# Second layer's vector work kept in two lists and split into halves; raw weight loads issued first in each slot

## Chip, cores and metric

One core of one Trainium2 chip runs the whole kernel. The metric is device time in microseconds, the median of several executions; lower is better. Engines are named as the profile names them: PE (TensorE matmuls) and PEld (its weight loads), DVE (VectorE), ACT (ScalarE), POOL (GpSimd), and SPq, the queue on SyncE that issues the transfers.

## What is computed

```python
# q, k, v: (4, 8, 576, 64); w_in (512, 2048), w_out (2048, 512)
# moe2: w_gate, w_val (512, 1536), w_out (1536, 512); all float32
ret = (scale * q @ k.T) * Dmat          # Dmat[i, j] = gamma_h ** (i - j) for i >= j, else 0
x = merge_heads(ret @ v)                # (2304, 512)
h = x @ moe_w_in
g = h * tanh(log1p(exp(min(h, 20))))    # for h > 20: h * tanh(h)
x = g @ moe_w_out                       # first layer
g, val = x @ w_gate, x @ w_val
out = (g * sigmoid(g) * val) @ w_out    # second layer
```

## The kernel before

The program has three parts. **Retention** runs over 20 steps of up to 128 positions and prepares the first weights beside it. **The first layer** runs over 96 slots (`slot`, line 570): six blocks of 384 tokens by 16 slices of the hidden width; block b and place i in it make slot s = 16 b + i. **The second layer** (lines 601 to 790) works on three data sets of 768 tokens, and on each in six units u, one for each pair of 128-wide slices of its hidden width.

Every float32 product is made of three matmuls on a high half (a rounded copy that ACT casts) and a low half (the rest, a subtract on DVE). This is why each operand costs a cast and a subtract.

A slot gives PE 12 matmuls of `g1` (bank `h`) and 12 of `g2`, the latter for the slot LAG = 4 earlier (they add up in four banks `acc`). ACT then makes Mish (`mish`) and the high half, DVE the low half (`halves`). In a block's places 12, 13 and 15, `split_hi` and `split_lo` make the parts `xs` of the next block's input. In place 3 of the next block `g2_out` copies the four `acc` banks out to `y`, two on ACT and two on DVE. Whatever follows in the slot comes last: `second(s)` (line 228).

`second` prepares the second layer's weights beside the first layer, in five-slot steps, one for each of 12 groups (gate or value of one pair), from slot PREP = 20 on. Stage 0 of `group` issues two raw loads (`rawg` or `rawv`), stage 1 rebiases, stage 2 joins words, stage 3 makes four combinations and stores three operands through tiles `c` (four buffers) to DRAM (`comb`), stage 4 stores the other four. `last` does the same for a row of the output weights (`rawf`): its load is issued in the group's stage-4 slot, behind the four stores, and its rebias (line 103, ACT and DVE) stands in the slot after that. All these transfers are issued by SP in program order; a store there waits for the subtract that fills its tile, and what stands behind it waits too.

The second layer multiplies with Strassen's scheme: seven products `t` (six matmuls each) for gate (z = 0) and seven for value (z = 1) make one unit of 14 steps. Two of the three banks `t` of a pass take more than one product, so a bank must be emptied on DVE or ACT (line 719, 758) before the next but one step writes it; there are only two buffers in `pha`:

```python
                p = t[tn]
                n = z * NG + c
...
                fins(FINS[c])
                if nexty and n >= 6:
                    next(nexty[0], None)
```

In the value pass, steps 2, 4, 5 and 6 each finish one quarter: DVE multiplies it into the gate (`sg`, line 734), ACT casts the high half, DVE subtracts the low half (`finish`, `halves`). The output matmuls `fa` (line 689, nine for each quarter) go into `ready`, which is handed to `finq` when the next unit begins; `fins` takes 3, 2, 3, 2, 3, 2, 3 of them after the seven steps of a pass, so 36 in a unit. A data set's seven operands `y` (Strassen's combinations of the first layer's output, split into high and low) are made by `ysteps`: for the first set in the first layer's last four slots, two steps a slot, and for the next ones in the last unit of the set before, one step after each product from n = 6 on. Each such step is one or two DVE instructions of 768 elements a partition and a cast of 768. Where y, `second` and the rest meet on an engine, the order of the program decides: engines work in order.

## Time and profile before

| | us |
|---|---|
| time, median of 3 runs (lowest, highest) | 959.03 (956.24, 960.19) |
| the profiled execution | 957.2 |
| its span | 955.4 |
| PE busy | 918.8 (96%) |
| DVE busy | 518.9 (54%) |
| ACT busy | 360.8 (38%) |
| POOL busy | 109.3 (11%) |

PE is the busiest engine, and the chain that ended last runs on it for 72% of the span. Busy shares are averages over the three parts; what PE waits for, and where, is in the rows below. [...]

### The profile page before, as it was taken

What the parts mean: (1) busy time and instruction counts of PE and PEld (TensorE: products, weight loads), DVE (VectorE), ACT (ScalarE), POOL (GpSimd) and SP (SyncE); (2) the same over time, 40 slices, a digit from 0 to 9 for tenths busy, and PEclk for the clock granted to TensorE, in tenths of its full rate; (3) what the DMA queues carried; (4) which work ended last, traced back from release to release, by engine and by line L of the source; (5) the groups of instructions that cost most, each with busy time, mean ns of one, the idle gap of its engine ahead of it and who ended that gap; (6) DMA issues with size and microseconds to landing.
All of it is one profiled execution on the core that took longest, in us unless ns stands there. A gap on an engine that the chain in (4) does not pass through costs nothing.

```text
span 955.4 us, 14669 instructions
## 1 busy us (share of the span) xinstructions
PE 918.8 (96%) x5684; PEld 869.6 (91%) x5684; DVE 518.9 (54%) x896; ACT 360.8 (38%) x731; POOL 109.3 (11%) x90
## 2 busy tenths in 40 slices
PE   8898999999999999998999999998999997999998
PEld 7777899999999899998999899987999995999997
DVE  3997796255666656556234444455544456544444
ACT  4776564344554444445334222223222223222221
POOL 3765443000100000000000000000000000000000
PEclk9999999999999999999999999999999999999999
DMA  9999453045555555564116755543645443644411
GB/s 230 257 254 235 133 161 98 1 143 166 182 172 190 181 194 179 174 191 149 45 67 246 242 206 210 198 154 110 220 156 159 167 159 98 220 167 154 157 64 67
DMA packets 115349, 156.57 MB, mean 164 GB/s; under 512 B 45392, under 2 KB 80976, under 8 KB 115280
## 3 DMA queue, kind: packets, MB, share of 16 engines
q1 hardware_dynamic: 114176, 155.21, 51.8%
q8 instruction: 45, 0.74, 0.3%
q10 hardware_dynamic: 1104, 0.42, 0.2%
q14 instruction: 24, 0.20, 0.1%
HBM read 122.58 MB, written 33.03 MB: 163 GB/s over the span
## 4 chain that ended last, share of the span: by engine, by line
PE 72%; DMA 9%; DVE 9%; ACT 4%; SPq 2%; issue 2%; POOL 1%; DVEq 0%; ACTq 0%
PE t L749 26%; PE h L510 15%; PE fa L689 15%; PE acc L544 15%; DMA k<-in_k_dram 3%; DMA rawf<-in_moe_w_out_dram 2%; DMA comb<-c 2%; DMA rawv<-in_moe_w_val_dram 1%; DVE y L619 1%; SPq L300 1%; DVE g L567 1%; ACT y L618 1%; DMA rawg<-in_moe_w_gate_dram 1%; DVE c L177 1%; DVE rawv L108 1%
## 5 line engine op out<-in xcount | busy, mean ns | idle before, releaser
L749 PE MATMUL t<-y,su 128*128 128x384 f32 x1512 | 308.5, 340 | 13.4 <-DVE v L719 4.7
L749 PEld LDWEIGHTS t<-y,su 128*128 128x128 f32 x1512 | 271.7, 188 | 40.1 <-DVE cv L719 7.1
L510 PE MATMUL h<-xs,u 128*128 128x384 f32 x1152 | 216.7, 337 | 3.8 <-DVE xs L250 3.2
L544 PE MATMUL acc<-g,u 128*128 128x384 f32 x1152 | 215.2, 336 | 2.4 <-ACT y L554 2.4
L510 PEld LDWEIGHTS h<-xs,u 128*128 128x128 f32 x1152 | 202.0, 189 | 5.3 <-DVE xs L250 4.2
L544 PEld LDWEIGHTS acc<-g,u 128*128 128x128 f32 x1152 | 201.6, 188 | 3.2 <-ACT y L554 2.7
L567 DVE TENSOR_TENSOR g<-m,g 128x384 fp32r<-128x384 f32 x96 | 53.7, 559 | 100.1 <-ACT g L566 98.6
L561 ACT ACTIVATE m<-h 128x384 f32<-128x384 f32 x96 | 46.7, 487 | 93.7 <-PE h L510 93.6
L726 ACT ACTIVATE sg<-sg 128x384 f32<-128x384 f32 x54 | 28.4, 525 | 98.8 <-DVE sg L719 98.8
L123 POOL TENSOR_TENSOR u<-raw,u 128x512 fp32r<-128x512 f32 x32 | 47.1, 1473 | 62.1 <-ACT u L122 60.3
L177 POOL TENSOR_TENSOR f<-rawf,f 128x256 fp32r<-128x256 f32 x24 | 23.0, 979 | 262.5 <-ACT f L176 262.5
L566 ACT CAST g<-m 128x384 fp32r<-128x384 f32 x96 | 49.4, 514 | 2.8 <-PE acc L544 0.2
L719 DVE TENSOR_TENSOR v<-t,p 128x384 f32<-128x384 f32 x36 | 20.0, 557 | 45.5 <-PE t L749 44.6
L719 DVE TENSOR_TENSOR u<-t,p 128x384 f32<-128x384 f32 x36 | 20.0, 557 | 44.7 <-PE t L749 43.2
L104 DVE TENSOR_SCALAR raw<-raw 128x512 uint32<-128x512 uint32 x32 | 37.7, 1178 | 0.0
L104 DVE TENSOR_SCALAR rawf<-rawf 128x512 uint32<-128x512 uint32 x12 | 5.2, 430 | 48.3 <-DMA rawf<-in_moe_w_out_dram 48.3
L734 DVE TENSOR_TENSOR sg<-sg,cv 128x384 f32<-128x384 f32 x54 | 30.2, 558 | 1.9
L122 ACT CAST u<-raw 128x512 fp32r<-128x512 f32 x32 | 21.2, 662 | 22.3 <-DVE raw L112 22.2
L103 ACT ACTIVATE rawf<-rawf 128x512 f32<-128x512 f32 x12 | 8.3, 689 | 56.5 <-DMA rawf<-in_moe_w_out_dram 56.5
L357 POOL TENSOR_TENSOR vs<-v,gv 128x512 f32<-128x512 f32 (+1 forms) x20 | 27.0, 1348 | 20.6 <-DMA v<-in_v_dram 16.2
L108 DVE SCALAR_TENSOR_TENSOR raw<-raw 128x512 uint32<-128x512 uint32 x32 | 26.2, 818 | 0.0
L112 DVE SCALAR_TENSOR_TENSOR raw<-raw 128x512 uint32<-128x512 uint32 x32 | 26.1, 816 | 0.0
(363 smaller groups left out, 1064.6 us busy)
## 6 DMA issues: line engine op xcount, KB each, us to landing
su<-comb SPq DMA_DIRECT2D x126, 512.0 KB, 3.3
comb<-c SPq DMA_DIRECT2D x84, 256.0 KB, 2.4
raw<-in_moe_w_in_dram SPq DMA_DIRECT2D x16, 512.0 KB, 4.8
raw<-in_moe_w_out_dram SPq DMA_DIRECT2D x16, 512.0 KB, 3.6
rawg<-in_moe_w_gate_dram SPq DMA_DIRECT2D x12, 512.0 KB, 6.7
rawf<-in_moe_w_out_dram SPq DMA_DIRECT2D x12, 512.0 KB, 4.8
rawv<-in_moe_w_val_dram SPq DMA_DIRECT2D x12, 512.0 KB, 6.2
find<-f SPq DMA_DIRECT2D x24, 256.0 KB, 2.4
```

The source lines that it names most:

```text
L104: nc.vector.tensor_scalar(lo, lo, 29, None, op0=ALU.logical_shift_right)
L108: nc.vector.scalar_tensor_tensor(lo, hi, 0x80000000, lo, op0=ALU.bitwise_and, op1=ALU.bitwise_or)
L123: nc.gpsimd.tensor_tensor(out=u[:, 1, :], in0=w, in1=u[:, 0, :].bitcast(F32), op=ALU.subtract)
L177: eng.tensor_tensor(out=c[:, 1, :], in0=x, in1=c[:, 0, :].bitcast(F32), op=ALU.subtract)
L510: nc.tensor.matmul(ps, lhsT=u[:, a, kk * 128:(kk + 1) * 128], rhs=s[:, e, :], start=(c == 0), stop=(c == n - 1),)
L544: nc.tensor.matmul(accs[b][d][:, :T], lhsT=u[:, a, d * 128:(d + 1) * 128], rhs=g[:, e, :], start=(i == 0 and c == 0), stop=(i == F1 - 1 an ...
L561: nc.scalar.activation(w, hs.pop(s), AF.Mish)
L566: nc.scalar.copy(out=g[:, 0, :], in_=x)
L567: nc.vector.tensor_tensor(out=g[:, 1, :], in0=x, in1=g[:, 0, :].bitcast(F32), op=ALU.subtract)
L689: nc.tensor.matmul(accs["f", b][m], lhsT=gs[u, e, h][:, x, m * 128:(m + 1) * 128], rhs=fu[2 * (u % PAIRS) + e][:, a, :], start=first, stop ...
L719: nc.vector.tensor_tensor(out=out_, in0=a, in1=b_, op=ALU.add)
L749: nc.tensor.matmul(p, lhsT=w[:, n % 2, a, kk * 128:(kk + 1) * 128], rhs=y[:, x, kk, :], start=begin and kk == 0 and (a, x) == (0, 0), stop ...
```

## The change

1. `second` skips places 3 and 14 of every block (list `free`): its steps move to later slots, and the last one goes from slot 82 to slot 90. In a slot, the stages run in the order of their number, so that a raw load comes ahead of stores, and a group's stages 1 and 2 come ahead of `last`'s stages 2 and 3.
2. In the second layer the multiply of steps 4 to 6, the cast and the low-half subtract go to a list `later`, and the next data set's y to a list `ahead`. After a step's bank is emptied and its `fa` matmuls are issued, up to two entries of `later` and one of `ahead` are issued; casts to a high half do not count.
3. y is made in halves of 384 elements a partition: 22 DVE instructions in place of 11. The first part (12 of them) stands in the unit before the last, the rest in the last unit's value pass and in the first four steps of the next unit. The temporary gets a tile of its own (`t2`) instead of one of the five `g`. For the first data set eight entries are issued in a slot.
4. A quarter's `fa` matmuls enter `finq` when its low half is issued, not when the next unit begins.

```diff
@@ -225,13 +225,20 @@
             for h in range(DM // KH):
                 put(x[:, h * KH:(h + 1) * KH], find[i][:, :, h * KH:(h + 1) * KH], f"f{i}_{h}", nc.gpsimd)
 
+    free = [s for s in range(PREP, NB * F1) if s % F1 not in (3, F1 - 2)]
+
     def second(s):
+        if s not in free:
+            return
+        now = []
         for n in range(2 * PAIRS):
-            t = s - PREP - 5 * n
+            t = free.index(s) - 5 * n
             if 0 <= t < 5:
-                group(n // 2, n % 2, t)
+                now.append((t, group, (n // 2, n % 2, t)))
             if 4 <= t < 8:
-                last(n, t - 4)
+                now.append((t - 4, last, (n, t - 4)))
+        for _, f, a in sorted(now, key=lambda x: x[0]):
+            f(*a)
 
     xt = {}
     x2t = {}
@@ -613,52 +620,58 @@
             nc.sync.dma_start(out=fu[i].bitcast(F32), in_=find[i])
 
 
-        def ysplit(n, c, x):
-            y = pools["y"].tile([128, 2, KT // 2, T], F32R, tag="y", name=f"y{n}_{c}")
-            nc.scalar.copy(out=y[:, 0], in_=x)
-            nc.vector.tensor_tensor(out=y[:, 1], in0=x, in1=y[:, 0].bitcast(F32), op=ALU.subtract)
-            ys[n, c] = y
 
         def ysteps(n):
             b = {(k + 1, e + 1): x2t[2 * n + e][:, 2 * k:2 * k + 2, :] for k in range(2) for e in range(2)}
+            tmp = pools["t2"].tile([128, 2, T], F32, tag="t2", name=f"t2_{n}")
 
             def minus(out_, a, b_):
-                nc.vector.tensor_tensor(out=out_, in0=a, in1=b_, op=ALU.subtract)
-
-            ysplit(n, 0, b[1, 1])
-            minus(b[1, 1], b[1, 2], b[1, 1])
-            yield
-            t2 = gp.tile([128, 2, T], F32R, tag="g", name=f"t2_{n}", bufs=LAG + 1).bitcast(F32)
-            minus(t2, b[2, 2], b[1, 1])
-            ysplit(n, 1, t2)
-            yield
-            ysplit(n, 2, b[2, 1])
-            minus(b[2, 1], b[2, 1], t2)
-            yield
-            minus(b[1, 2], b[2, 2], b[1, 2])
-            ysplit(n, 3, b[1, 2])
-            yield
-            ysplit(n, 4, b[1, 1])
-            yield
-            ysplit(n, 5, b[2, 1])
-            yield
-            ysplit(n, 6, b[2, 2])
-            yield
-
-        y0 = None
+                def half(k):
+                    nc.vector.tensor_tensor(out=out_[:, k], in0=a[:, k], in1=b_[:, k], op=ALU.subtract)
+                return [lambda k=k: half(k) for k in range(KT // 2)]
+
+            def split(c, x):
+                def high():
+                    y = pools["y"].tile([128, 2, KT // 2, T], F32R, tag="y", name=f"y{n}_{c}")
+                    nc.scalar.copy(out=y[:, 0], in_=x)
+                    ys[n, c] = y
+
+                def rest(k):
+                    y = ys[n, c]
+                    nc.vector.tensor_tensor(out=y[:, 1, k], in0=x[:, k], in1=y[:, 0, k].bitcast(F32), op=ALU.subtract)
+
+                return high, [lambda k=k: rest(k) for k in range(KT // 2)]
+
+            h0, r0 = split(0, b[1, 1])
+            h1, r1 = split(1, tmp)
+            h2, r2 = split(2, b[2, 1])
+            h3, r3 = split(3, b[1, 2])
+            h4, r4 = split(4, b[1, 1])
+            h5, r5 = split(5, tmp)
+            h6, r6 = split(6, b[2, 2])
+            t1 = minus(b[1, 1], b[1, 2], b[1, 1])
+            t2 = minus(tmp, b[2, 2], b[1, 1])
+            t3 = minus(b[1, 2], b[2, 2], b[1, 2])
+            t4 = minus(tmp, b[2, 1], tmp)
+            return [h0] + r0 + t1 + t2 + [h1] + t3 + r1 + t4, [[h2] + r2, [h3] + r3, [h4] + r4, [h5] + r5, [h6] + r6]
+
+        y0 = []
         for s in range(2, NS):
             slot(s)
             if s == NS - 5:
                 cr.close()
                 pools["y"] = ctx.enter_context(tc.tile_pool(name="yp", bufs=9, side="right", reuse_waits="tile"))
                 pools["sg"] = ctx.enter_context(tc.tile_pool(name="sg", bufs=5, side="right", reuse_waits="tile"))
+                pools["t2"] = ctx.enter_context(tc.tile_pool(name="t2", bufs=1, side="right", reuse_waits="tile"))
                 pools["sa"] = ctx.enter_context(tc.tile_pool(name="sa", bufs=SA, side="right", reuse_waits="tile"))
                 for n in range(SA):
                     stream(n)
-                y0 = ysteps(0)
+                ya, yb = ysteps(0)
+                y0 = ya + [f for fs in yb for f in fs]
             elif y0:
-                next(y0, None)
-                next(y0, None)
+                for f in y0[:8]:
+                    f()
+                y0 = y0[8:]
         for s in range(NS - LAG, NS):
             g2(s)
             g2_out(s)
@@ -673,8 +686,9 @@
 
 
         sg = {}
-        ready = []
         finq = []
+        later = []
+        ahead = []
 
         def fins(count):
             while count and finq:
@@ -702,12 +716,23 @@
         def finish(u, e, h):
             i = u % PAIRS
             k = (e, h)
-            halves(sg.pop((u, e, h)), (u, e, h))
             start = i == 0 and k in ((0, 0), (1, 1))
             stop = i == PAIRS - 1 and k in ((1, 0), (0, 1))
-            lst = order(TT, stop)
-            for n, (m, a, x, c) in enumerate(lst):
-                ready.append((u, e, h, m, a, x, start and c == 0, stop and c == 2))
+
+            def high():
+                x = sg[u, e, h]
+                gs[u, e, h] = gp.tile([128, 2, T], F32R, tag="g", name=f"g{u}_{e}{h}", bufs=LAG + 1)
+                nc.scalar.copy(out=gs[u, e, h][:, 0, :], in_=x)
+
+            def rest():
+                x = sg.pop((u, e, h))
+                g = gs[u, e, h]
+                nc.vector.tensor_tensor(out=g[:, 1, :], in0=x, in1=g[:, 0, :].bitcast(F32), op=ALU.subtract)
+                for m, a, d, c in order(TT, stop):
+                    finq.append((u, e, h, m, a, d, start and c == 0, stop and c == 2))
+
+            later.append(high)
+            later.append(rest)
 
 
         def strassen(u, z):
@@ -731,7 +756,10 @@
                         x = pools["sg"].tile([128, T], F32, tag="cv", name=f"cv{u}_{e}{h}", bufs=2)
                         add(x, bank_, part_)
                     y = sg[u, e, h]
-                    nc.vector.tensor_tensor(out=y, in0=y, in1=x, op=ALU.mult)
+                    if part_ is None:
+                        nc.vector.tensor_tensor(out=y, in0=y, in1=x, op=ALU.mult)
+                    else:
+                        later.append(lambda: nc.vector.tensor_tensor(out=y, in0=y, in1=x, op=ALU.mult))
                     finish(u, e, h)
 
             for c, (nm, tn, begin, end) in enumerate((
@@ -771,22 +799,29 @@
                 else:
                     result(0, 1, p, r["u"])
                 fins(FINS[c])
-                if nexty and n >= 6:
-                    next(nexty[0], None)
+                k = u % PAIRS * 2 * NG + n - (PAIRS - 1) * 2 * NG - 8
+                if 0 <= k < 5 and u + 1 < NS2:
+                    ahead.extend(yb[k])
+
+                for todo_, m in ((later, 2), (ahead, 1)):
+                    while todo_ and m:
+                        f = todo_.pop(0)
+                        f()
+                        m -= f.__name__ != "high"
 
         FINS = (3, 2, 3, 2, 3, 2, 3)
         for u in range(NS2):
-            finq += ready
-            ready.clear()
-            nexty = []
-            if u % PAIRS == PAIRS - 1 and u + 1 < NS2:
-                nexty.append(ysteps(u // PAIRS + 1))
+            i = u % PAIRS
+            if i == PAIRS - 2 and u + 2 < NS2:
+                ya, yb = ysteps(u // PAIRS + 1)
+                ahead += ya
             if u + 1 < PAIRS:
                 fin_load(2 * u + 2)
                 fin_load(2 * u + 3)
             for z in range(2):
                 strassen(u, z)
-        finq += ready
+        while later:
+            later.pop(0)()
         fins(len(finq))
```

In the stage-4 slot of the group whose output row is `rawf5`, SP's queue had these rows (`c2_8` to `c2_13` are the four tiles of stage 4, `c2_7` to `c2_12` ahead of them the three of stage 3):

```order
L178 DMA comb2_3_89<-c2_7_3430 128x512
L178 DMA comb2_4_90<-c2_9_3434 128x512
L178 DMA comb2_6_92<-c2_12_3438 128x512
L178 DMA comb2_4_90<-c2_8_3472 128x512
L178 DMA comb2_5_91<-c2_10_3476 128x512
L178 DMA comb2_5_91<-c2_11_3480 128x512
L178 DMA comb2_6_92<-c2_13_3484 128x512
L171 DMA rawf5_3488<-in_moe2_w_out_dram 128x1024
L171 DMA rawg3_0_3522<-in_moe2_w_gate_dram 128x4x256
```

and has now:

```order
L178 DMA comb2_3_89<-c2_7_3559 128x512
L178 DMA comb2_4_90<-c2_9_3563 128x512
L178 DMA comb2_6_92<-c2_12_3567 128x512
L171 DMA rawf5_3601<-in_moe2_w_out_dram 128x1024
L178 DMA comb2_4_90<-c2_8_3603 128x512
L178 DMA comb2_5_91<-c2_10_3607 128x512
L178 DMA comb2_5_91<-c2_11_3611 128x512
L178 DMA comb2_6_92<-c2_13_3615 128x512
L171 DMA rawg3_0_3649<-in_moe2_w_gate_dram 128x4x256
```

The load of `rawf5` has moved ahead of four stores; the loads of the next group stay behind them.

On DVE, the value pass of unit 5 (the last of the first data set), from the emptying `u5_1` of step 1 to the emptying `cv5_01` of step 6; `y` on the left of an arrow is an operand or a combination of the next data set. Before:

```order
L719 TENSOR_TENSOR u5_1_6433<-t5_1_2_6426,p15_1_6416 128x384
L619 TENSOR_TENSOR y1_2_6437<-y2_3556,y1_2_6437 128x768
L626 TENSOR_TENSOR y2_3556<-y2_3556,t2_1_6421 128x768
L734 TENSOR_TENSOR sg5_00_6348<-sg5_00_6348,t5_1_1_6407 128x384
L567 TENSOR_TENSOR g(5, 0, 0)_6450<-sg5_00_6348,g(5, 0, 0)_6450 128x384
L626 TENSOR_TENSOR y3_4237<-y3_4237 128x768
L619 TENSOR_TENSOR y1_3_6457<-y3_4237,y1_3_6457 128x768
L719 TENSOR_TENSOR v5_1_6466<-t5_1_2_6426,p15_1_6416 128x384
L619 TENSOR_TENSOR y1_4_6470<-y2_3556,y1_4_6470 128x768
L719 TENSOR_TENSOR cv5_11_6482<-t5_1_3_6473,v5_1_6466 128x384
L734 TENSOR_TENSOR sg5_11_6372<-sg5_11_6372,cv5_11_6482 128x384
L567 TENSOR_TENSOR g(5, 1, 1)_6485<-sg5_11_6372,g(5, 1, 1)_6485 128x384
```

and now:

```order
L744 TENSOR_TENSOR u5_1_6465<-t5_1_2_6458,p15_1_6453 128x384
L641 TENSOR_TENSOR y1_2_6469<-y2_3516,y1_2_6469 128x384
L760 TENSOR_TENSOR sg5_00_6389<-sg5_00_6389,t5_1_1_6444 128x384
L730 TENSOR_TENSOR g5_00_6484<-sg5_00_6389,g5_00_6484 128x384
L641 TENSOR_TENSOR y1_2_6469<-y2_3516,y1_2_6469 128x384
L744 TENSOR_TENSOR v5_1_6494<-t5_1_2_6458,p15_1_6453 128x384
L641 TENSOR_TENSOR y1_3_6498<-y3_4179,y1_3_6498 128x384
L744 TENSOR_TENSOR cv5_11_6510<-t5_1_3_6501,v5_1_6494 128x384
L762 TENSOR_TENSOR sg5_11_6413<-sg5_11_6413,cv5_11_6510 128x384
L730 TENSOR_TENSOR g5_11_6516<-sg5_11_6413,g5_11_6516 128x384
L641 TENSOR_TENSOR y1_3_6498<-y3_4179,y1_3_6498 128x384
L744 TENSOR_TENSOR cv5_10_6526<-t5_1_2_6458,p15_1_6453 128x384
```

Between two emptyings there is now one instruction of 384 for the next set where there were one or two of 768, and the rest of these instructions has moved to the units on either side.

On PE, the value pass of unit 0, its steps 2 to 5 (`t0_1_*` are the products, `g(0, 0, 0)` or `g0_00` is the quarter that step 2 finishes). Before:

```order
L749 MATMUL t0_1_1_5474<-y0_2_5249,su4_5387 128x384 x6
L749 MATMUL t0_1_2_5485<-y0_3_5254,su5_5389 128x384 x6
L749 MATMUL t0_1_3_5514<-y0_4_5287,su5_5389 128x384 x6
L749 MATMUL t0_1_2_5485<-y0_5_5290,su6_5391 128x384 x6
L749 MATMUL t0_1_3_5514<-y0_6_5323,su6_5391 128x384 x6
L749 MATMUL t1_0_1_5559<-y0_0_5210,su7_5393 128x384 x6
```

and now:

```order
L777 MATMUL t0_1_1_5488<-y0_2_5260,su4_5401 128x384 x6
L777 MATMUL t0_1_2_5499<-y0_3_5294,su5_5403 128x384 x6
L703 MATMUL fa0_0_5528<-fu0_5411,g0_00_5517 128x512 x2
L777 MATMUL t0_1_3_5533<-y0_4_5298,su5_5403 128x384 x6
L703 MATMUL fa0_1_5529<-fu0_5411,g0_00_5517 128x512 x2
L703 MATMUL fa0_2_5530<-fu0_5411,g0_00_5517 128x512
L777 MATMUL t0_1_2_5499<-y0_5_5302,su6_5405 128x384 x6
L703 MATMUL fa0_2_5530<-fu0_5411,g0_00_5517 128x512
```

The `fa` matmuls of a quarter stand one product behind it, where they had stood behind the whole unit.

## Rows read from the trace of the kernel before

**Rows 1.** The page's busy time, share of the span and count for each engine.

```profile
PE 918.8 (96%) x5684; PEld 869.6 (91%) x5684; DVE 518.9 (54%) x896; ACT 360.8 (38%) x731; POOL 109.3 (11%) x90
```

**Rows 2.** The page's groups, PE: busy, mean ns | idle before, what ended it.

```profile
L749 PE MATMUL t<-y,su 128*128 128x384 f32 x1512 | 308.5, 340 | 13.4 <-DVE v L719 4.7
...
L510 PE MATMUL h<-xs,u 128*128 128x384 f32 x1152 | 216.7, 337 | 3.8 <-DVE xs L250 3.2
L544 PE MATMUL acc<-g,u 128*128 128x384 f32 x1152 | 215.2, 336 | 2.4 <-ACT y L554 2.4
```

**Rows 3.** Windows of 25 us: busy by engine, then clock, DMA share, GB/s.

```profile
300.00:325.00 25.00, 22.57 (x121) 21.72 (x120) 15.70 (x31) 11.85 (x28) 2.93 (x4) 0.95 0.48 158
325.00:350.00 25.00, 25.00 (x144) 25.00 (x143) 16.89 (x33) 12.10 (x27) 3.02 (x3) 0.98 0.53 179
...
650.00:675.00 25.00, 23.78 (x115) 21.74 (x115) 13.21 (x23) 6.93 (x13) 0.00 (x0) 0.93 0.41 137
```

**Rows 4.** Timeline of PE where data sets change: start, us, instruction [idle before <-releaser].

```profile
649.72 1.99 PE L749 MATMUL t<-y,su 128*128 128x384 f32 x6 [2.37 <-DVE v L719]
```

**Rows 5.** The same timeline at the second change of data sets.

```profile
797.41 1.31 PE L749 MATMUL t<-y,su 128*128 128x384 f32 x6 [2.36 <-DVE v L719]
```

**Rows 6.** Timeline of PE in the first layer, where a block's banks are emptied.

```profile
320.81 3.07 PE L544 MATMUL acc<-g,u 128*128 128x384 f32 x12 [2.37 <-ACT y L554]
```

**Rows 7.** Timeline of SPq, DVE, PE and ACT just ahead of that.

```profile
307.62 1.09 DVE L177 TENSOR_TENSOR c<-rawv,c 128x256 fp32r<-128x256 f32 x3
...
312.00 2.25 PE L510 MATMUL h<-xs,u 128*128 128x384 f32 x12
...
312.92 0.44 SPq L171 DMA_DIRECT2D rawf<-in_moe_w_out_dram  x1
...
318.76 0.69 ACT L103 ACTIVATE rawf<-rawf 128x512 f32<-128x512 f32 x1 [5.84 <-DMA rawf<-in_moe_w_out_dram]
```

**Rows 8.** The tile rawf: flight of its 12 loads, from issue to landing.

```profile
DMA to landing us min/median/max: 3.7/4.8/6.0
```

**Rows 9.** ACT's waits from 150 to 526 us: total, times, longest.

```profile
ACT rawf L103 <- DMA rawf<-in_moe_w_out_dram: 56.5, 12, 6.0
ACT c L176 <- DMA comb<-c: 24.5, 28, 5.0
```

**Rows 10.** Groups by shape on DVE: y's low half (768), the quarters' low half (384).

```profile
L567 DVE TENSOR_TENSOR g<-m,g 128x384 fp32r<-128x384 f32 x96 | 53.7, 559 | 100.1 <-ACT g L566 98.6 <-PE h L510 1.5
...
L619 DVE TENSOR_TENSOR y<-y,y 128x768 fp32r<-128x768 f32 x18 | 17.1, 956 | 6.9 <-ACT y L618 6.8
```

**Rows 11.** Timeline of an undisturbed unit's value pass, steps 2 and 3.

```profile
593.13 1.22 PE L749 MATMUL t<-y,su 128*128 128x384 f32 x6
...
594.98 0.51 ACT L566 CAST g(3, 0, 0)_6063<-sg 128x384 fp32r<-128x384 f32 x1 [3.39 <-DVE sg L734]
595.52 0.56 DVE L567 TENSOR_TENSOR g(3, 0, 0)_6063<-sg,g(3, 0, 0)_6063 128x384 fp32r<-128x384 f32 x1 [0.58 <-ACT g(3, 0, 0)_6063 L566]
595.77 0.19 PEld L689 LDWEIGHTS fa<-fu,g(2, 1, 0)_5917 128*128 128x128 f32 x1
```

**Rows 12.** The same unit, steps 4 to 6 and the next unit's step 1.

```profile
597.66 0.56 DVE L719 TENSOR_TENSOR cv<-t,v 128x384 f32<-128x384 f32 x1 [0.96 <-PE t L749]
...
599.39 0.56 DVE L567 TENSOR_TENSOR g(3, 1, 1)_6091<-sg,g(3, 1, 1)_6091 128x384 fp32r<-128x384 f32 x1 [0.58 <-ACT g(3, 1, 1)_6091 L566]
...
599.87 0.55 DVE L719 TENSOR_TENSOR cv<-t,p 128x384 f32<-128x384 f32 x1
...
602.07 0.55 DVE L719 TENSOR_TENSOR cv<-t,u 128x384 f32<-128x384 f32 x1
...
603.20 1.04 PE L749 MATMUL t<-y,su 128*128 128x384 f32 x5
```

**Rows 13.** Timeline of SPq: loads of the output weights; below it their flight.

```profile
515.71 1.75 SPq L613 DMA_DIRECT2D fu<-find  x4
```

**Rows 14.** The tile fu: flight of its 12 loads.

```profile
DMA to landing us min/median/max: 3.6/5.2/7.1
```

## Prediction

> **What bounds the kernel now.** I read the busy shares first: PE works for 918.8 of 955.4 us [rows 1], so what can be won is PE's idle time and its slow stretches, and the next view is what PE waited for. In the page's groups the second layer's products `t` wait 13.4 us in all, for DVE; the first layer's `h` waits 3.8 us, mostly for `xs`, and its `acc` 2.4 us for a copy by ACT [rows 2]. The rest of PE's idle time lies in the retention part, which the change does not touch. The windows of 25 us then tell what the clock lost: 0.95 and 0.98 behind the wait for `acc`, 0.93 at the first change of data sets [rows 3], so 25 x 0.07 = 1.75 us at each of the two places. The clock had fallen behind a wait of 2.37 us, where six matmuls then took 1.99 us [rows 4]; behind one of 2.36 us at the second change they took 1.31 [rows 5], so such a wait brings the fall only at times. An undisturbed unit shows DVE ending a chain in time, and no wait on PE [rows 11, 12]. So the waits sit in two places: where the next data set's y is made inside a value pass, and where the first layer's blocks change.
>
> **Second layer: waits that go.** The waits of `t` lie at the two changes of data sets [rows 4, 5] and, a small part, in unit 0's value pass, whose steps carry no `fa` matmuls before and now carry some. At the changes the cause is the same each time: an emptying of a bank stands on DVE behind a low half of 768 elements, itself behind a cast. The change leaves one half of 384 between two emptyings at most, and puts 12 of a set's 22 halves into a unit that had no such work. I take away 13.4 us. Six matmuls behind a wait take 1.31 to 1.33 us and 1.22 otherwise [rows 5, 11]; eleven waits make 11 x 0.1 = 1.1 us. With the waits goes what the clock lost behind them, 1.75 us.
>
> **Second layer: what is late next.** In the last unit's value pass each step still gets one half. In an undisturbed unit the emptyings of steps 4, 5 and 6 start at 597.66, 599.87 and 602.07: DVE needs 2.2 us a step where PE takes (603.20 - 593.13) / 6 = 1.68, and falls back [rows 11, 12]. The last emptying ends at 602.07 + 0.55 = 602.62, and the next pass's step 1, which writes that bank, starts at 603.20: 0.58 us of cover. From the end of a low half to the next emptying DVE issues every 0.48 us (599.39 to 599.87), so the halves behind steps 4 and 5 move the last emptying by 2 x 0.48 = 0.96 us, and the cast of 768 that step 5 issues by some 0.3 us more. That is 0.96 + 0.3 - 0.58 = 0.7 us of wait, at two changes: 1.4 us. The halves behind steps 1 to 3 and in the unit before fall where DVE waits for PE (0.96 us ahead of 597.66). Bounds: none (the halves fit the cover), and all of what PE waited before.
>
> The halves cost more in sum: 2 x 0.559 in place of 0.956 us [rows 10], 0.16 us a pair, 3.6 us for the 22 pairs of two sets; they are hidden where the last paragraph says. [...]
>
> **Second layer: output matmuls one product behind their quarter.** This is a new dependence: `fins` keeps its pace of 36 a unit, but now finds the list empty by the end of step 2 in each unit, and step 3's two `fa` matmuls read a high half just cast. In the undisturbed unit, the product ends at 593.13 + 1.22 = 594.35, the cast ends at 594.98 + 0.51 = 595.49, and the weights for the first `fa` of step 3 load at 595.77 [rows 11]: 0.28 us to spare. The low half (ends 596.08) is first read two steps later. I take no cost in 17 units. In unit 0 steps 0 to 2 have no `fa`, so the chain of 595.49 - 594.35 = 1.14 us and a weight load of 0.19 [rows 11] stand against six matmuls alone, about 1.1 us (half of 2.25 [rows 7]): a wait of some 0.3 us. The tail stays PE's: 26 instead of 36 matmuls after the last product, the other ten earlier. The output weights are now read after unit 0's eleventh product, 11 x 1.05 = 11.5 us into the second layer and not after its fifteenth; their loads issue as it starts, at 515.71 [rows 13], and fly at most 7.1 us [rows 14], which leaves 4 us.
>
> **First layer.** The wait of 2.37 us [rows 6] reads back so: ACT sat 5.84 us for `rawf`, whose load SP issued at 312.92 [rows 7], behind four stores that wait for DVE. PE's product `h`, which ACT's next Mish needs, had ended at 314.25 [rows 7]. Now the load stands behind stage 3's three stores alone. The last of their subtracts ends at 308.71 [rows 7], so the issue comes near 309.2, 3.7 us earlier, and at the same flight the data lands at 315.1, 0.8 us behind `h`. All that hung on it, the copies among it, moves forward by 3.7 us, more than 2.37. The wait for `xs` at the end of block 1 follows such a stall too. The other one, at the end of block 4, comes from combinations and stores of places 13 and 14; place 14 is now free, and the input's split in place 15 has a slot of 24 matmuls, some 4.2 us, to itself. I take 3.8 + 2.4 = 6.2 us away, and 1.75 us of clock.
>
> The skipped slots push the preparation from slot 82 to 90; the tiles of the second layer that take its room are asked for in slot 91, and its first product comes behind four more slots, over 16 us later. Other phases now meet the block changes, such as four combinations and three stores in place 2 of block 2, and a rebias in place 2 of block 5. Nothing in the trace prices them there; bounds are 0 and one more 2.37 us wait, and I take 0.5.
>
> **The sum.** Gone: 13.4 + 1.1 + 1.75 + 6.2 + 1.75 = 24.2 us. New: 1.4 + 0.3 + 0.5 = 2.2. The span falls by 22.0 to 933.4, the profiled execution from 957.2 to 935.2. The median of the runs lies 1.8 above that execution; I give **937**.
>
> **The rivals.** The first layer's waits stay: the loads leave earlier, but compete with the stores behind them, or a later phase meets the next block change. For it: all 12 rebiases waited, 56.5 us in sum, and the flight varies from 3.7 to 6.0 us [rows 8, 9]. Against: 3.7 us of lead. Time: 937 + 6.2 + 1.75 - 0.5 = 944.5.
>
> DVE stays the bound at the changes of data sets: 10 of the 22 halves still stand in the value pass and the steps behind it. If half the old waits and clock loss remain, (13.4 + 1.1 + 1.75) / 2 = 8.1 instead of 1.4: 943.7. Both together come to 951.
>
> Slower: the output matmuls run dry in each unit. Place: step 3 of 18 value passes. The cover is 0.28 us; each microsecond that ACT's cast is later than that costs 18 us. From (22 + 4.8 + 0.5) / 18 = 1.5 us of wait in each unit, the kernel ends over 0.5% slower, near 964. For it: a chain of three instructions on two engines must end inside one product. Against: [rows 11] show this chain with both its ends, and the change leaves DVE's order in an undisturbed unit as it was.
>
> Stores delayed: the load of 512 KB now goes first, so four stores land later, and ACT waits for the tiles `c` (24.5 us before [rows 9]). The next cast into them comes two slots and more later, 8 us, against a flight of 4.8. [...] If it decided, it would undo the first layer's gain: the first rival's time, and its chance is in that rival's.
>
> **How the numbers follow.** Forecast (932 to 941): 0.60. First layer stays: 0.13. DVE stays: 0.12. Both, or another loss that leaves about the old time: 0.06. Slower: 0.05. Below 932, with no new wait and something I did not see: 0.04. A range of 932 to 946 takes in the forecast and most of the first two rivals, and the bounds of the new waits (none: 957.2 - 24.2 = 933). What a measurement of this kernel can tell from no change is about 0.5%, 4.8 us; the runs before spread over 4. Faster by more than that: 0.60 + 0.13 + 0.12 + 0.04 and a third of the 0.06, 0.91; same 0.04; slower 0.05.
>
> **What would show it.** Right: waits of `t` for DVE near 2 us, with what is left at step 1 of the first pass of a new data set; no waits of `h` and `acc`; clock 1.00 from 200 us on; ACT's waits for `rawf` well under 56.5 us; DVE busy a few microseconds longer. Wrong: `fa` waiting for the cast `g` once a unit; `t` waiting for `cv` at the changes; `acc` waiting for `y` in place 4 of a block.

## Result and profile after

The changed kernel takes 934.05 us (median of 4 runs, 932.93 to 935.65) against 959.14 before (four runs, one more than in the table above); the ratio is 0.9744, with a 95% interval from 0.9719 to 0.9770. The forecast was 937, in a range from 932 to 946.

From the page of the changed kernel, its span, its busy shares and PE's groups for the products `t`, for `h` and for `acc` (busy, mean ns | idle before, what ended it); they answer to [rows 1, 2]:

```profile
span 932.5 us, 14692 instructions
PE 912.3 (98%) x5684; PEld 867.8 (93%) x5684; DVE 520.2 (56%) x929; ACT 362.3 (39%) x731; POOL 108.6 (12%) x90
...
L777 PE MATMUL t<-y,su 128*128 128x384 f32 x1512 | 306.5, 338 | 1.0 <-DVE cv L744 1.0
L517 PE MATMUL h<-xs,u 128*128 128x384 f32 x1152 | 214.6, 336 | 0.0
L551 PE MATMUL acc<-g,u 128*128 128x384 f32 x1152 | 214.6, 336 | 0.9 <-ACT y L561 0.9
```

The idle time ahead of `t` fell from 13.4 to 1.0 us, that ahead of `h` from 3.8 to nothing, that ahead of `acc` from 2.4 to 0.9. DVE is no less busy (520.2 us against 518.9). The windows that answer to [rows 3] have the clock at 1.00, in the first layer and at the change of data sets, as all other windows of 25 us from 200 to 925 us have in both kernels:

```profile
300.00:325.00 25.00, 25.00 (x145) 25.00 (x144) 15.27 (x32) 11.87 (x26) 2.24 (x2) 1.00 0.45 140
...
625.00:650.00 25.00, 24.49 (x127) 22.24 (x126) 14.60 (x29) 8.64 (x15) 0.00 (x0) 1.00 0.46 148
650.00:675.00 25.00, 25.00 (x131) 23.26 (x130) 13.32 (x25) 6.19 (x13) 0.00 (x0) 1.00 0.66 225
```

To split the gain I cut the span at two places of PE's timeline, the first `acc` product and the second layer's first product. Before:

```profile
116.52 2.24 PE L544 MATMUL acc<-g,u 128*128 128x384 f32 x12
...
515.52 9.76 PE L749 MATMUL t<-y,su 128*128 128x384 f32 x55
```

After:

```profile
117.84 2.24 PE L551 MATMUL acc<-g,u 128*128 128x384 f32 x12
...
508.82 11.71 PE L777 MATMUL t<-y,su 128*128 128x384 f32 x66
```

| stretch | before | after | change |
|---|---|---|---|
| start to first `acc` | 116.5 | 117.8 | +1.3 |
| first `acc` to second layer ("first layer" below) | 399.0 | 391.0 | -8.0 |
| second layer to the end | 439.9 | 423.7 | -16.2 |
| span | 955.4 | 932.5 | -22.9 |

The first stretch is retention, which the change leaves alone; in the twelve profiles of this case it ended between 116.5 and 119.0, so its 1.3 us are within its spread. PE waited longer for loads of `k` here (8.5 us against 5.7), but only 5.0 in the profile where the stretch ended last, so what makes it vary stays open. The median fell by 2 us more than the span, since the profiled execution of before lay below its median.

What is left of the waits of `t` are two, one at each change of data sets. DVE's timeline around the first (start, us, instruction, idle before) with ACT's cast and PE's product:

```profile
638.58 0.56 DVE L744 TENSOR_TENSOR cv<-t,v 128x384 f32<-128x384 f32 x1 [0.18 <-PE t L777]
...
640.79 0.55 DVE L641 TENSOR_TENSOR y<-y,y 128x384 fp32r<-128x384 f32 x1
641.26 0.55 DVE L744 TENSOR_TENSOR cv<-t,p 128x384 f32<-128x384 f32 x1
...
642.86 0.83 ACT L636 CAST y<-y 128x768 fp32r<-128x768 f32 x1
...
643.72 0.56 DVE L641 TENSOR_TENSOR y<-y,y 128x384 fp32r<-128x384 f32 x1 [0.18 <-ACT y L636]
644.20 0.55 DVE L744 TENSOR_TENSOR cv<-t,u 128x384 f32<-128x384 f32 x1
...
644.80 1.33 PE L777 MATMUL t<-y,su 128*128 128x384 f32 x6 [0.51 <-DVE cv L744]
```

The three emptyings of steps 4, 5 and 6 now lie 2.68 and 2.94 us apart, where an undisturbed unit has 2.2 [rows 12]: a half of `y` stands ahead of the second and the third, and the third's half also waits 0.18 us for a cast. The next pass's step 1 then waits 0.51 us. This is the step that the prediction named.

### The profile page after: what moved, and what is told of

Its sections match the earlier page's. It is cut to its first block, busy times and chain, and to the rows that moved or that the text cites. A ratio compares the mean times of both kernels' runs of the same rounds, so it can differ in the third digit from the quotient of the medians.

```text
span 932.5 us, 14692 instructions
## 1 busy us (share of the span) xinstructions
PE 912.3 (98%) x5684; PEld 867.8 (93%) x5684; DVE 520.2 (56%) x929; ACT 362.3 (39%) x731; POOL 108.6 (12%) x90
## 4 chain that ended last, share of the span: by engine, by line
PE 88%; DMA 5%; DVE 3%; ACT 2%; SPq 1%; issue 1%; POOL 0%; ACTq 0%; DVEq 0%; POOLq 0%
PE t L777 28%; PE acc L551 20%; PE h L517 20%; PE fa L703 16%; DMA k<-in_k_dram 4%; PE o L436 1%; PE o L443 1%; DMA rawg<-in_moe_w_gate_dram 1%; PE tk L360 1%; PE s L376 1%; PE state L412 0%; DMA comb<-c 0%; DMA q<-in_q_dram 0%; SPq L91 0%; DVE p L385 0%
## 5 line engine op out<-in xcount | busy, mean ns | idle before, releaser
L703 PE MATMUL fa<-fu,g 128*128 128x512 f32 x648 | 190.0, 395 | 0.1
L703 PEld LDWEIGHTS fa<-fu,g 128*128 128x128 f32 x648 | 118.6, 188 | 7.5 <-ACT g L725 0.5
L725 ACT CAST g<-sg 128x384 fp32r<-128x384 f32 x72 | 36.9, 513 | 175.0 <-DVE sg L762 121.4
L730 DVE TENSOR_TENSOR g<-sg,g 128x384 fp32r<-128x384 f32 x72 | 40.2, 558 | 40.6 <-ACT g L725 40.6
L177 POOL TENSOR_TENSOR f<-rawf,f 128x256 fp32r<-128x256 f32 x24 | 23.4, 992 | 284.3 <-ACT f L176 284.3
```

The source lines that it names most:

```text
L703: nc.tensor.matmul(accs["f", b][m], lhsT=gs[u, e, h][:, x, m * 128:(m + 1) * 128], rhs=fu[2 * (u % PAIRS) + e][:, a, :], start=first, stop ...
L725: nc.scalar.copy(out=gs[u, e, h][:, 0, :], in_=x)
L730: nc.vector.tensor_tensor(out=g[:, 1, :], in0=x, in1=g[:, 0, :].bitcast(F32), op=ALU.subtract)
```

## Experiments

Each kernel was run beside the kernel before, whose medians there were 958.2 to 958.7 us; the ratios are to those. Stretches and idle times come from one profile of each kernel. The columns of stretches are cut as above; idle is PE's for `h` and `acc`, and for `t` and `fa`, in us, with the number of waits.

| kernel | median | ratio to before (95%) | first layer | idle | second layer | idle |
|---|---|---|---|---|---|---|
| before | 959.14 | | 399.0 | 6.1 (4) | 439.9 | 13.3 (11) |
| changed | 934.05 | 0.9744 (0.9719 to 0.9770) | 391.0 | 0.9 (1) | 423.7 | 1.0 (2) |
| first part only | 950.24 | 0.9911 (0.9884 to 0.9938) | 391.3 | 0.7 (1) | 439.9 | 14.5 (12) |
| second part only | 943.60 | 0.9835 (0.9811 to 0.9858) | 400.3 | 5.2 (4) | 423.6 | 1.0 (2) |
| no skipped places | 936.11 | 0.9769 (0.9748 to 0.9791) | 393.4 | 2.4 (3) | 423.6 | 1.0 (2) |
| loads behind stores | 934.67 | 0.9748 (0.9730 to 0.9766) | 391.5 | 1.1 (2) | 423.6 | 1.0 (2) |
| whole y | 937.82 | 0.9778 (0.9751 to 0.9805) | 390.3 | none | 427.2 | 4.2 (4) |
| output matmuls a unit late | 935.85 | 0.9762 (0.9740 to 0.9784) | 391.5 | 0.9 (1) | 425.9 | 2.1 (6) |
| cast three times | 946.97 | 0.9883 (0.9860 to 0.9906) | 390.7 | 0.6 (1) | 438.1 | 11.2 (20) |
| y at its old place | 944.87 | 0.9859 (0.9828 to 0.9889) | 390.5 | 0.4 (1) | 433.6 | 8.9 (6) |
| fifth tile c, halves moved | 931.60 | 0.9729 (0.9714 to 0.9744) | 389.7 | none | 422.2 | none |
| changed, once more | 933.31 | 0.9738 (0.9721 to 0.9754) | 390.0 | none | 423.7 | 1.0 (2) |

### The two parts alone

The first kernel has the new `second` in the old program; the other has the old `second` in the new one:

```diff
 # second part only: against the changed kernel
-    free = [s for s in range(PREP, NB * F1) if s % F1 not in (3, F1 - 2)]
     def second(s):
-        if s not in free:
-            return
...
+            t = s - PREP - 5 * n
```

> Only the first layer's part of the change is in (places 3 and 14 skipped, stages in the order of their number); the second layer is as before. Theory: the two parts are independent, and a wait costs its idle time, 0.17 us of overlap between matmuls and 0.1 us of restart. The stretch from the first acc to the second layer's first product falls from 396.9 to about 389 us as in the changed kernel, the waits of t stay at about 13.4 us, and the time is near 951 (8 less than before). Rival: the two parts lean on each other (the first layer's late steps push the second layer), and this kernel gains less than 5 us.

> Only the second layer's part is in (two lists, halves, output matmuls fed at once); the preparation in the first layer is as before. Theory: the waits of t fall to about 1 us, the waits of h and acc stay at about 6 us, the second layer takes 423 to 424 us in place of 439.9, and the time is near 943 (16 less than before). Rival: the parts are not additive; then this and the kernel with the first part alone do not sum to 25 us.

Both came out as the first theory has it (the 396.9 and 389 us of the first expectation count from PE's next group, 2.1 us behind the first `acc`; counted from where the table starts they are 399.0 and 391.0): 950.2 and 943.6, and 8.4 and 15.0 us below the 958.6 that the kernel before had beside them; the sum, 23.4, is near the 25 of both together. In the kernel with the first part alone, the waits of `t` stayed and even grew (PE, whom it waited for: total, times, longest):

```profile
PE t L756 <- DVE cv L726: 5.6, 6, 1.4
PE t L756 <- DVE v L726: 4.7, 2, 2.4
PE t L756 <- DVE u L726: 3.1, 2, 1.6
PE t L756 <- DVE sg L741: 1.1, 2, 0.5
```

That is 14.5 us where the kernel before has 13.3, while its second layer takes the same 439.9 us and its clock did not fall (1.00 in the window where [rows 3] have 0.93). My reading is that while PE is slow, DVE catches up, and the stretch at the lower clock stands for one more wait of `cv`; no run forces the clock to test it.

The kernel with the second part alone shows what the first layer's waits cost when the clock falls behind two of them:

```profile
300.00:325.00 25.00, 22.87 (x122) 22.05 (x121) 15.52 (x31) 12.29 (x29) 2.73 (x3) 0.94 0.48 158
...
425.00:450.00 25.00, 22.55 (x120) 21.98 (x119) 15.10 (x30) 11.70 (x27) 1.85 (x2) 0.93 0.57 184
```

Its first layer takes 400.3 us with 5.2 us of idle time; the kernel before, with 6.1 us but one fall less, took 399.0.

### Which half of the first part

```diff
 # no skipped places
-    free = [s for s in range(PREP, NB * F1) if s % F1 not in (3, F1 - 2)]
+    free = list(range(PREP, NB * F1))
 # loads behind stores
-        for _, f, a in sorted(now, key=lambda x: x[0]):
+        for _, f, a in now:
```

> The changed kernel without the skipped places: preparation runs in every slot, but loads go first. Theory (the load's lead is the cause): waits of h and acc together under 1.5 us, ACT's waits for rawf under 5 us, time within 2 us of the changed kernel's 934. Rival (the free places are the cause): h or acc wait 3 us or more at the block changes, and the time is 938 or more.

> The changed kernel without the new order in a slot: places 3 and 14 are skipped, but the raw load stands behind the stores again. Theory (the load's lead is the cause): ACT waits for rawf some 50 us again, and where a rebias falls in place 0, 1 or 2 of a block acc waits 2 us or more at least once; time 936 to 940. Rival (the free places are the cause): no waits of h and acc beyond 1 us, time 934.

Here my theory fell. With the loads first but no free places, `h` and `acc` wait 2.4 us together, more than the 1.5 that I allowed (and less than the 3 of the rival), and the first layer takes 393.4. With free places and the loads behind the stores, it takes 391.5, within 0.5 us of the changed kernel, and the time is 934.7. In the seven profiles of kernels that have both measures, the first layer took 390.0 to 391.5 us, with at most one wait of 0.9: the kernel without free places lies outside that spread, the one without the new order at its edge. The intervals of their two times overlap, so this rests on the traces. ACT's waits for the stores' tiles `c` and for the three kinds of raw load in these two kernels (total, times, longest), first without free places:

```profile
ACT c L176 <- DMA comb<-c: 28.8, 27, 3.8
ACT rawv L103 <- DMA rawv<-in_moe_w_val_dram: 21.9, 12, 3.9
ACT rawg L103 <- DMA rawg<-in_moe_w_gate_dram: 16.9, 10, 3.4
ACT rawf L103 <- DMA rawf<-in_moe_w_out_dram: 8.9, 12, 1.6
```

and with the loads behind the stores:

```profile
ACT rawf L103 <- DMA rawf<-in_moe_w_out_dram: 46.0, 12, 5.3
...
ACT c L176 <- DMA comb<-c: 13.0, 24, 2.2
...
ACT rawv L103 <- DMA rawv<-in_moe_w_val_dram: 3.7, 3, 2.2
ACT rawg L103 <- DMA rawg<-in_moe_w_gate_dram: 2.6, 2, 2.2
```

The load's lead does take away most of ACT's wait for `rawf`, but much of it comes back at the group's own loads, which still stand behind four stores: 47.7 us against 52.3 in sum. And those 52.3 us, 46 of them for `rawf`, cost PE 1.1 us once places 3 and 14 carry no step. What counts is where a wait of ACT falls, not how long all of them are. One pair shows it at the same place: in the kernel with the loads behind the stores, too, one rebias falls in place 2 of a block (block 5), and PE hardly waits for the copies behind it, where it waited 2.37 us [rows 6, 7]:

```profile
450.15 0.67 ACT L103 ACTIVATE rawf<-rawf 128x512 f32<-128x512 f32 x1 [4.48 <-DMA rawf<-in_moe_w_out_dram]
...
452.18 1.00 PE L551 MATMUL acc<-g,u 128*128 128x384 f32 x4 [0.25 <-ACT y L561]
```

ACT's own wait is 1.36 us shorter there as well (4.48 against 5.84), so the pair is no clean measure. Skipping the places also moves all later steps to other places; no run tells the free places from the moved steps, or place 3 from place 14. Each of the two measures alone takes away most of the first layer's waits (5.6 and 7.5 of 8.0 us of its stretch); they overlap.

### Which part of the second

```diff
 # whole y: one instruction of 768 where there are two of 384
-                return [lambda k=k: half(k) for k in range(KT // 2)]
+                return [lambda: nc.vector.tensor_tensor(out=out_, in0=a, in1=b_, op=ALU.subtract)]
...
 # output matmuls a unit late: a quarter's go into a list that is handed over when the next unit begins
-                    finq.append((u, e, h, m, a, d, start and c == 0, stop and c == 2))
+                    ready.append((u, e, h, m, a, d, start and c == 0, stop and c == 2))
...
+            finq += ready
+            ready.clear()
...
 # y at its old place: all of it from step 6 of the last unit's gate pass on, up to three halves a step
-            if i == PAIRS - 2 and u + 2 < NS2:
+            if i == PAIRS - 1 and u + 1 < NS2:
...
+                if k == -2 and u + 1 < NS2:
+                    ahead.extend(ya)
...
-                for todo_, m in ((later, 2), (ahead, 1)):
+                for todo_, m in ((later, 2), (ahead, 3)):
```

> The changed kernel with y made in whole pieces of 768 again (11 instructions in place of 22 for a data set), in the same two lists and the same units. Theory (spreading and halving both count): behind steps 4 and 5 stand pieces of 0.96 in place of 0.55 us, so the last emptying comes 2 x 0.4 = 0.8 us later than with halves and the next pass's step 1 waits 0.5 + 0.8 = 1.3 us or somewhat more at each of two changes; waits of t 2.5 to 5 us, time 936 to 939. Rival A (halving is everything): waits near the old 13.4 us, time 948. Rival B (halves only cost: 3.6 us more work on DVE): no more waits than with halves, time 934.

> The changed kernel with the output matmuls of a unit handed over when the next unit begins, as before. Theory (0.28 us of cover hold): reading a quarter one product behind it costs nothing in 17 units, so this gains nothing there; in unit 0's value pass the steps lose their output matmuls again, and the waits for the emptied banks return there (0.7 us of idle, some 1.2 with overlap and restart). Time 935 to 936. Rival (the fresh dependence costs a little in every unit): 18 x 0.1 us or more is won, time under 933.

> The changed kernel with all of the next data set's y made where it was made before (from the last unit's step 6 of the gate pass to the end of its value pass), in halves, up to three in a step behind the emptying. Theory (spreading over two more units is what counts): three halves of 0.48 us in each step of the value pass make DVE some 3.6 us a step against PE's 1.7, and waits of t return to 8 to 13 us; time 944 to 950. Rival (placing them behind the emptyings, in small pieces, is what counts): waits under 4 us, time under 938.

All three follow the first theory in kind and, but for the output matmuls, in size. In whole pieces, the second layer takes 3.5 us more, in two waits at each change; PE at the first:

```profile
643.72 1.33 PE L775 MATMUL t<-y,su 128*128 128x384 f32 x6 [0.80 <-DVE cv L742]
647.06 1.32 PE L775 MATMUL t<-y,su 128*128 128x384 f32 x6 [1.31 <-DVE cv L742]
```

The wait of step 1 has the 1.3 us that were expected; the 0.80 ahead of it, at step 0 of the same pass, I had not seen coming. With y at its old place, though in halves and behind the emptyings, 9.9 of the 16.2 us come back:

```profile
636.45 0.73 PE L703 MATMUL fa<-fu,g 128*128 128x512 f32 x2 [1.01 <-ACT g L725]
644.39 1.33 PE L777 MATMUL t<-y,su 128*128 128x384 f32 x6 [1.59 <-DVE cv L744]
648.26 1.32 PE L777 MATMUL t<-y,su 128*128 128x384 f32 x6 [1.85 <-DVE cv L744]
```

So spreading the work over three units is the largest part; undoing the small pieces cost 3.5 us and undoing the early output matmuls 2.2 (some 1.2 were expected), each with the rest in place. The list `later` was not taken out by itself. Of the 2.2 us, two waits come from unit 0: without `fa` between its products PE runs ahead of DVE, and unit 1's first two products wait for their banks again, as they did before:

```profile
524.75 1.32 PE L778 MATMUL t<-y,su 128*128 128x384 f32 x6 [0.48 <-DVE cv L745]
526.95 1.33 PE L778 MATMUL t<-y,su 128*128 128x384 f32 x6 [0.18 <-DVE cv L745]
```

The other two, 0.19 and 0.18 us, are for ACT's copy of a bank, in the second unit of each later data set (at 669.16 and 809.87); why they come there stays open:

```profile
PE t L778 <- ACT p L787: 0.4, 2, 0.2
```

### The cover of the new dependence

```diff
+                for _ in range(3 if k == (0, 0) else 1):
                     nc.scalar.copy(out=gs[u, e, h][:, 0, :], in_=x)
```

> The changed kernel with the high half of step 2's quarter cast three times instead of once in each unit (the same values written again). That makes ACT's chain 2 x 0.42 = 0.84 us longer ahead of step 3's output matmuls. Theory (the slower rival's mechanism is real and its cover is 0.28 us): each unit waits 0.84 - 0.28 = 0.56 us, and with overlap and restart 0.83; 18 units make 10 us of idle and 15 us of time: 946 to 950. Rival (these matmuls have slack that the rows did not show): fewer than 3 us of waits, time under 938.

Each of the 18 units waits, 10.1 us in sum as expected (PE from 130 us on):

```profile
PE fa L703 <- ACT g L726: 10.1, 18, 1.2
```

The parts differ from the expectation, though. Unit 0, which has no cover, waits 1.22 us and the other 17 wait 0.52 or 0.53. And three casts take 1.60 us where one takes 0.51 [rows 11], so the chain grew by 1.09 us and not by 0.84 (0.42 us is what a cast of 256 elements takes in these traces, not one of 384). One of the 17:

```profile
592.57 1.60 ACT L726 CAST g<-sg 128x384 fp32r<-128x384 f32 x3 [3.39 <-DVE sg L761]
...
594.22 0.30 PEld L703 LDWEIGHTS fa<-fu,g 128*128 128x128 f32 x2 [0.84 <-ACT g L726]
594.23 0.73 PE L703 MATMUL fa<-fu,g 128*128 128x512 f32 x2 [0.52 <-ACT g L726]
```

The weight load, which waits for nothing at this place of the changed kernel, waits 0.84 us here for a chain that is 1.09 longer: the cover is 0.25 us, against the 0.28 of the prediction. That the mean wait of 0.56 us equals 0.84 less 0.28 is luck. The second layer grows by 14.4 us, more than its 10.2 us of added idle time: the rest is 4.2 / 18 = 0.24 us for each wait. The slower rival was thus a real mechanism, with about the price that was put on it, and the change stays some 0.25 us clear of it.

### A further step

```diff
-        pools["c"] = cr.enter_context(tc.tile_pool(name="pc", bufs=4, side="right"))
+        pools["c"] = cr.enter_context(tc.tile_pool(name="pc", bufs=5, side="right"))
...
-                for todo_, m in ((later, 2), (ahead, 1)):
+                for todo_, m in ((later, 2), (ahead, (2, 2, 1, 2, 0, 0, 0)[c] if u % PAIRS == PAIRS - 1 and z or u % PAIRS == 0 and not z else 1)):
```

> The changed kernel with a fifth tile c (stores hold ACT back less, so the group's loads leave earlier) and with the halves of the last unit moved off steps 4 to 6 of its value pass: two behind steps 1 and 3, one behind step 2, two behind steps 0, 1 and 3 of the next pass. Theory: the two waits of t (1.0 us in all) go, the wait of acc (0.9) goes or halves, and with 0.27 us each for overlap and restart the time falls by 1.5 to 2.5 us against the changed kernel run beside it: about 932. Rival: the halves moved make the next unit's step 1 or 4 wait instead, and the fifth tile changes nothing: 934.

> The changed kernel once more, beside the previous one on the same chip, for their difference. All theories: 933 to 935 us.

PE waits for nothing in either layer any more. The second layer takes 422.2 us against 423.7, which is the 1.0 us of idle time and the price of two waits; the median is 931.6 against 933.3 of the changed kernel on the same chip. The intervals of the two ratios overlap (0.9714 to 0.9744 and 0.9721 to 0.9754), so the times alone don't show the 1.7 us; the trace shows the second layer's 1.4 of them, and the first layer's 0.3 are within its spread. What the fifth tile does is open: the changed kernel had no wait of `acc` in its second profile either.

## Why the prediction was right, and where it was not

**The second layer's waits that go**: right. 13.4 us fell to 1.0, for the named reason. The 1.75 us for the clock fit the sum, though not as a cost of their own: the first part alone shows the same stretch with no fall of the clock and one wait more. The small part that the prediction places in unit 0's value pass lies just behind it, at the first two products of unit 1 (84 matmuls of `t` stand ahead of the wait at 531.27 of the kernel before); the cause was the named one.

**The price of a wait**: mis-sized, the largest error in the two layers' terms. I charged 0.1 us for the restart beside the idle time. The runs with many waits show 0.24 (18 waits of the cast) to 0.28 (ten waits more with the first part alone: 16.3 us of stretch for 13.5 of idle). With few waits it scatters: 0.16 with whole y (two waits more), 0.3 with late output matmuls (four), 0.5 with y at its old place (four: 9.9 us of stretch for 7.9 of idle), so a quarter of a microsecond is a mean and not a constant. The idle time of the profile begins where the last matmul ends, and undisturbed matmuls start ahead of that, as two rows of the changed kernel show:

```profile
642.37 1.22 PE L777 MATMUL t<-y,su 128*128 128x384 f32 x6
...
643.43 0.86 PE L703 MATMUL fa<-fu,g 128*128 128x512 f32 x3
```

The product ends at 643.59, and the next group has started 0.16 us before; by my reading, behind a wait this overlap is lost as well as the 0.1 us of restart (six matmuls take 1.33 us at 644.80 and 1.22 at 642.37), 0.26 us together. With 0.25 the second layer's 16.2 us come to 12.3 of idle, 9 x 0.25 = 2.3, and 1.75, 16.3 in sum; the forecast had 14.5. The first layer's 8.0 us come to 5.2, 3 x 0.25 = 0.75, and 1.75, 7.7 in sum; the forecast had 7.45.

**From the span to the median**: the largest single part of the 3 us between 937 and 934.05, and no part of the mechanism. The prediction added 1.8 us because the profiled execution of the kernel before lay that far below its median; that of the changed kernel (934.33) lay 0.3 above. This made 2.1 us, the second layer 1.7 and the first 0.5; retention took 1.3 back.

**What is late next**: right in place and cause. The halves and the cast moved the last emptying by 2.68 + 2.94 - 4.41 = 1.21 us (the forecast: 1.26), and the wait was 0.5 us (the forecast: 0.7).

**Output matmuls behind their quarter**: no cost in 17 units was right, and the slowed cast showed a cover of 0.25 us for the 0.28 of the prediction. In unit 0 I expected 0.3 us of wait; there was none beyond 0.1. The early matmuls also removed the waits for the banks behind unit 0; handing them over late again cost 2.2 us in all.

**The first layer**: the size was right (7.45 against 8.0), the cause only in part, so that the size came out is in part luck. I put the gain down to the load's lead of 3.7 us. The lead is there: ACT waited 2.3 us for `rawf`, not 56.5 [rows 9]. But the group's loads took its place, as one stretch of the changed kernel's timeline shows (SPq, ACT and PE at the start of block 4):

```profile
371.99 0.42 SPq L171 DMA_DIRECT2D rawf<-in_moe_w_out_dram  x1
...
375.67 1.58 SPq L171 DMA_DIRECT2D rawg<-in_moe_w_gate_dram  x2
...
382.25 0.69 ACT L103 ACTIVATE rawg<-rawg 128x512 f32<-128x512 f32 x1 [4.46 <-DMA rawg<-in_moe_w_gate_dram]
...
385.68 2.50 PE L551 MATMUL acc<-g,u 128*128 128x384 f32 x12 [0.91 <-ACT y L561]
```

ACT sits 4.46 us for `rawg`, the copies of `acc` queue behind it, and PE waits 0.91 us: the same chain as [rows 6, 7] with another load, inside the bounds that I gave for new phases, though I had named other places. And the runs without one or the other measure show that the skipped places, with the steps that they move, matter more than the order: the order alone left 2.4 us of waits and 393.4 us, the skipped places alone 1.1 and 391.5. The failed step is "all that hung on it moves forward by 3.7 us": I followed one load and not the next two in the same queue.

**The signs**: two that stand under "wrong" came, in small: `t` waits for `cv` at both changes (1.0 us), where a wait was also forecast, and `acc` waits for `y` in place 4 of block 4 (0.91 us). DVE's busy time grew by 1.3 us and not by a few; each half took 0.55 us, near the 0.559 of [rows 10], and other groups took less.

**The rivals**: neither of the two that keep part of the waits came true. Of the rival of the delayed stores, the mechanism came true and the price did not. Stores do land later (4.0 us against 2.4, the median of 84), and it is the order that does it. Without free places but with the loads first:

```profile
comb<-c SPq DMA_DIRECT2D x84, 256.0 KB, 4.3
```

and with free places but the loads behind the stores:

```profile
comb<-c SPq DMA_DIRECT2D x84, 256.0 KB, 2.4
```

All nine kernels with the loads first have 3.3 to 4.3 us, the three others 2.4. ACT's waits for tiles `c` still fell from 24.5 [rows 9] to 15.3 us, by the free places: 28.8 us without them and 13.0 without the new order. PE does not pay for the longer flight here: the kernel with the short one takes 934.7 us, the changed kernel 934.05. By what path the order lengthens the flight was not shown.

## What to carry to other kernels

When work for the next data set must share an engine with the emptying of banks, as `y` does DVE here, spread it over more units first, cut it into pieces next, and put each piece behind an emptying; undoing the first cost 9.9 us here and undoing the second 3.5, where all of the second layer's part was worth 16.2; the third was not undone by itself. ACT's waits for transfers mattered here by what was queued behind them at that place: keeping two places of each block free, which also moved the steps behind them, did more (7.5 of the first layer's 8.0 us) than issuing the loads earlier (5.6). And a wait on PE cost its idle time plus about a quarter of a microsecond in the mean (0.24 and 0.28 us in the comparisons with ten waits or more).

## What the runs showed of the hardware that was not expected

- Back-to-back matmuls overlap in the profile (by 0.16 us at 643.43 of the changed kernel), and a wait cost more than its idle time: 0.24 and 0.28 us in the two comparisons with ten waits or more, 0.16 to 0.5 in those with two or four.
- Behind waits of nearly the same length the clock fell in some places and runs and not in others: in the kernel before, to 0.93 in the window from 650 us, behind 2.37 us at 649.72 [rows 3, 4], while the windows from 775 to 825 us, with 2.36 us at 797.41 [rows 5], have 1.00; with the first part alone, where the longest waits are 2.4 us too, all windows from 200 to 925 us have 1.00. At the first change of data sets, where it fell, one wait for DVE fewer followed, and the second layer took the same time.
- With the 512 KB loads issued ahead of the 256 KB stores in SP's queue, the stores' median flight was between 3.3 and 4.3 us (nine kernels), with the loads behind them 2.4 (three).
